# Causal attention before two expert layers: half-empty transposed blocks put together by two, and a first pair loaded in parts

## The chip, the cores and the metric

The kernel runs on one core of one Trainium2 chip. The metric is device time in microseconds (us); a lower number is better. One core has five engines with a queue each: PE (matmul), DVE (vector), ACT (scalar), POOL (GpSimd) and SP, which here only issues loads and stores.

## The reference

```
scores = q @ k.T / sqrt(64)            # 2 batches x 12 heads, 448 x 448, float32
scores = where(key > query, -1e9, scores)
attn   = exp(scores - max) / (sum + 1e-9)
x      = (attn @ v), heads side by side # 896 tokens x 768
x      = relu(x @ w_in)**2 @ w_out      # 768 -> 2048 -> 768
h      = x @ w_in2
out    = (h - tanh(h)) @ w_out2
```

## The kernel before

Attention goes by 12 **pairs** of heads (6 pairs a batch). The 448 queries and the 448 keys are cut into 7 blocks of 64. For query block `c` only keys 0 to c are computed, `64*(c+1)` columns, so the seven blocks of a pair have 64 to 448 columns. The two heads of a pair lie on the two halves of the 128 partitions.

`scores` (L264) makes a pair's scores in two steps of two banks (`STEPS`, L54). Its matmuls use a quarter of the array each (64 rows, 64 columns), and four run beside each other: head j takes row half j, and the two banks of a step take the two column halves, so in one bank of the two the heads lie exchanged (`TURNED`). `maxes` (L287, DVE) reads a block's scores, adds the mask, writes it to the SBUF tile `p` and takes the row maximum; `exps` (L305, ACT) makes the exponentials and their sums; `small`, `sums`, `recips`, `norms` (DVE) divide by the sum.

`transposes` (L335, PE) then turns `p` block by block, 128 keys x 64 queries x 2 heads at a time: query block c with 64*(c+1) keys takes one transpose for each begun 128 keys, 16 in all, of which the last of blocks 0, 2, 4 and 6 is half empty (zeros, written once at L252). They go into four PSUM banks of four, and `tcopy` (L342, ACT) copies each bank, 512 columns, to `pt`. `pv` (L348, PE) multiplies with the values: for each 128 keys one matmul a head over all query blocks that see them, 448, 320 and 192 columns with 128 rows, and 64 columns with 64 rows for the last keys. Two heads run beside each other on the two column halves. A float32 matmul shows as two passes in the trace. `xhi` (ACT) and `xlo` (DVE) take the result apart into `x`.

The order of the work is written out by hand: iteration s of the loop at L549 makes the scores of pair s, the norms of pair s-1, and transposes, copies and product of pair s-2, each engine strictly in the order of the code. From s = 8 on (`f`), PE also gets the first six groups of the first expert layer's matmuls for batch 0 (`fill`), 18 matmuls a pair. DVE and ACT take a weight's passes in between (`w_prep`: shift, merge, high, split on DVE, one `w_exp` on ACT, L107), by a budget of 700 a pair; `late` runs the ACT pass that a DVE pass put off. After the loop come the four matmul stages of the expert layers, three matmuls for each product (L387 to L389).

At the start, `load_qk(0)` sends q on SP's queue and k on ACT's, nine `warm` matmuls follow on PE, and SP loads pairs 1 and 2, all values of batch 0 with the last 64 keys of both batches (`vend`), and the first weight.

Of the kernel before, what the change touches and what calls it, by code (L numbers as in the profile page):

```python
# [52 lines left out]

STEPS = (((6,), (5, 0)), ((3, 2), (4, 1)))  # L54
SOFF = {6: 0, 5: 0, 0: 384, 3: 0, 2: 256, 4: 0, 1: 320}
SI = {c: i for i, c in enumerate(c for st in STEPS for cs in st for c in cs)}
TURNED = {c for st in STEPS for c in st[1]}
# [6 lines left out]
TBASE = {kc: TBLK.index((kc, 2 * kc)) for kc in range(4)}  # L64
# [3 lines left out]
def body(ctx: ExitStack, tc: tile.TileContext, qT, kT, vL, w1, w2, w3, w4, out):  # L68
# [5 lines left out]
    mask = sb.tile([P, S], F32, name="mask")  # L74
# [127 lines left out]
    def load_qk(n):  # L202
        if n < NPAIR:
            b, hp = divmod(n, NP)
            qk[n] = (tmp(f"q{n}"), tmp(f"k{n}", "w"))
            nc.sync.dma_start(out=qk[n][0], in_=qT[b, hp])
            (nc.scalar if n == 0 else nc.sync).dma_start(out=qk[n][1], in_=kT[b, hp])

    def load_v(b):
        t = sb.tile([P, 3, DM], F32, tag=f"v{b}", name=f"v{b}")  # L210
        nc.sync.dma_start(out=t, in_=vL[b, : 3 * P].rearrange("(t p) d -> p t d", p=P))
        if b == 0:
            vs["end"] = slot(7, [D, B, DM], F32, "vend")
            nc.sync.dma_start(out=vs["end"], in_=vL[:, 3 * P :].rearrange("b p d -> p b d"))
        vs[b] = [t[:, 0], t[:, 1], t[:, 2], vs["end"][:, b]]
# [10 lines left out]
    warm(9)  # L226
# [4 lines left out]
    for j in range(2):  # L231
        r = mask[D * j : D * j + D, S - D :]
        nc.gpsimd.affine_select(out=r, in_=r, compare_op=ALU.is_ge, fill=-8e9, base=0, pattern=[[-1, D]], channel_multiplier=1)
# [3 lines left out]
    load_v(0)  # L237
    w_load(0)
# [9 lines left out]
    prob = [slot(i, [P, 2048], F32, f"p{i}") for i in range(3)]  # L248
    for i in range(3):
# [10 lines left out]
    def step(n, t):  # L260

        return STEPS[1 - t if n == 0 else t]

    def scores(n, t):  # L264
        q, k = qk[n]
        banks = []
        for z, cs in enumerate(step(n, t)):

            tag, bufs = ("s", 4) if n != 1 else ("t", 2) if t == 0 else ("oh"[z], 1)
            bank = ps.tile([P, 512], F32, tag=tag, bufs=bufs, name=f"s{n}_{t}_{z}")  # L270
            banks.append(bank)
            for c in cs:
                sc[n, c] = bank[:, SOFF[c] : SOFF[c] + D * (c + 1)]
        for i in range(2):
            for z, cs in enumerate(step(n, t)):
                for c in cs[i : i + 1]:
                    for j in range(2):
                        r, e = slice(D * j, D * j + D), D * (j ^ z)
                        nc.tensor.matmul(sc[n, c][e : e + D], lhsT=q[r, D * c : D * c + D], rhs=k[r, : D * (c + 1)], start=(c == cs[0]), stop=(c == cs[-1]), skip_group_check=True)  # L279
        if t == 1:  # L280
            qk.pop(n)
            load_qk(n + 3)

    def blocks(n, t):
        return [c for cs in step(n, t) for c in cs]

    def maxes(n, t, part=slice(None)):  # L287
# [4 lines left out]
        for c in cs[part]:  # L292
# [4 lines left out]
                in1=mask[:, S - w :],  # L297
# [37 lines left out]
    def transposes(n, t):  # L335
        tag, bufs = ("h", 1) if t == 2 and n < NP else ("t", 2)
        bank = tb[n, t] = ps.tile([P, 512], F32, tag=tag, bufs=bufs, name=f"t{n}_{t}")
        for i, (kc, c) in enumerate(TBLK[4 * t : 4 * t + 4]):
            o = bank.rearrange("p (i j q) -> p i j q", j=2, q=D)[:, i, :: -1 if c in TURNED else 1]
            nc.tensor.transpose(o, prob[n % 3][:, POFF[c] + P * kc : POFF[c] + P * kc + P], ident)  # L340

    def tcopy(n, t):  # L342
        if t == 0:
            pt[n] = slot(3 + n % 2, [P, 16, P], F32, f"pt{n}")
# [3 lines left out]
    def pv(n, kcs):  # L348
        b, hp = divmod(n, NP)
        if 0 in kcs:  # L350
            ob[n] = ps.tile([P, 512], F32, tag="o", bufs=1, name=f"o{n}")
        o = ob[n]
        for kc in kcs:
            r = P if kc < 3 else D
            m = NQ - 2 * kc
            for j in range(2):
                h = 2 * hp + j
                nc.tensor.matmul(  # L358
                    o[D * j : D * j + D, P * kc : S],
                    lhsT=vs[b][kc][:r, D * h : D * h + D],  # L360
                    rhs=pt[n][:r, TBASE[kc] : TBASE[kc] + m, D * j : D * j + D],
                    start=(kc == 0),
                    stop=(kc == 3),
                    skip_group_check=True,
                )
        if 3 in kcs:
# [182 lines left out]
    for s in range(NPAIR + 2):  # L549
# [26 lines left out]
        late()  # L576
# [12 lines left out]
        if a >= 1:  # L589
            xlo(a - 1)  # L590
        if f and ss:
# [29 lines left out]
        if sa:  # L621
            pv(a, range(4))
        if not ss:
            pump()
        late()
        if s == 1:
            warm(5, "s", 4)
        if s in (2, 3):
            w_load(s - 1)
        if s == 4:  # L630
            load_v(1)
    xhi(NPAIR - 1)
# [57 lines left out]
```

## Time and profile before

| what | value |
|---|---|
| median of 3 runs | 554.47 us (553.4 to 555.22) |
| the profiled execution's own time | 554.28 us |
| its span in the profile | 552.4 us |
| PE busy | 544.5 us (99%) |
| DVE, ACT busy | 347.6 us (63%), 330.0 us (60%) |
| chain that ended last | PE 93%, ACT 6%, DVE 1% |

The span is what the instructions cover; the 1.9 us between it and the time lie around the program. The shares of busy time are means over stages that differ: the pairs of the first batch fill about the first 45 us, those of the second batch the time to about 100 us, and the expert layers the rest.

### The profile page before, as it was taken

What the parts mean: (1) busy time and instruction counts of PE and PEld (TensorE: products, weight loads), DVE (VectorE), ACT (ScalarE), POOL (GpSimd) and SP (SyncE); (2) the same over time, 40 slices, a digit from 0 to 9 for tenths busy, and PEclk for the clock granted to TensorE, in tenths of its full rate; (3) what the DMA queues carried; (4) which work ended last, traced back from release to release, by engine and by line L of the source; (5) the groups of instructions that cost most, each with busy time, mean ns of one, the idle gap of its engine ahead of it and who ended that gap; (6) DMA issues with size and microseconds to landing.
All of it is one profiled execution on the core that took longest, in us unless ns stands there. A gap on an engine that the chain in (4) does not pass through costs nothing.

```text
span 552.4 us, 7889 instructions
## 1 busy us (share of the span) xinstructions
PE 544.5 (99%) x3038; PEld 480.9 (87%) x3038; DVE 347.6 (63%) x742; ACT 330.0 (60%) x630; POOL 1.6 (0%) x9
## 2 busy tenths in 40 slices
PE   8999999999999999999999999999999999999997
PEld 4667777899999999999999999999999999999996
DVE  5999998364534244453554688987654588887311
ACT  6999987577424266665333388776553677865100
POOL 1000000000000000000000000000000000000000
PEclk9999999999999999999999999999999999999999
DMA  8844223353443333331324130113755301016111
GB/s 259 299 149 132 109 82 97 108 171 115 135 152 115 114 115 114 115 114 58 114 66 163 58 115 1 57 58 90 237 188 171 114 1 58 0 59 217 55 50 51
DMA packets 15525, 61.85 MB, mean 112 GB/s; under 512 B 1664, under 2 KB 6400, under 8 KB 15488
## 3 DMA queue, kind: packets, MB, share of 16 engines
q1 hardware_dynamic: 15200, 61.00, 33.2%
q8 instruction: 24, 0.39, 0.3%
q10 hardware_dynamic: 288, 0.34, 0.2%
q14 instruction: 13, 0.11, 0.1%
HBM read 58.59 MB, written 2.75 MB: 111 GB/s over the span
## 4 chain that ended last, share of the span: by engine, by line
PE 93%; ACT 6%; DVE 1%; issue 0%; DVEq 0%
PE h L387 14%; PE h L389 14%; PE h L388 14%; PE o L387 14%; PE o L388 14%; PE o L389 14%; ACT p L312 3%; PE o L358 3%; PE t L340 2%; PE s L279 2%; ACT pt L346 2%; PE warm L224 1%; ACT raw L107 0%; DVE p L294 0%; ACT x L371 0%; DVE p L333 0%
## 5 line engine op out<-in xcount | busy, mean ns | idle before, releaser
L387 PE MATMUL o<-g,w 128*128 128x448 f32 x384 | 140.4, 366 | 0.0
L388 PE MATMUL o<-g,w 128*128 128x448 f32 x384 | 140.4, 366 | 0.0
L389 PE MATMUL o<-g,w 128*128 128x448 f32 x384 | 140.2, 365 | 0.0
L387 PEld LDWEIGHTS o<-g,w 128*128 128x128 f32 x384 | 72.1, 188 | 6.1
L389 PEld LDWEIGHTS o<-g,w 128*128 128x128 f32 x384 | 72.1, 188 | 6.0
L388 PEld LDWEIGHTS o<-g,w 128*128 128x128 f32 x384 | 72.1, 188 | 5.8
L387 PE MATMUL h<-x,w 128*128 128x448 f32 x192 | 72.3, 377 | 0.0
L388 PE MATMUL h<-y,w 128*128 128x448 f32 x192 | 70.6, 368 | 0.0
L389 PE MATMUL h<-y,w 128*128 128x448 f32 x192 | 70.6, 368 | 0.0
L389 PE MATMUL h<-x,w 128*128 128x448 f32 x192 | 70.6, 368 | 0.0
L387 PE MATMUL h<-y,w 128*128 128x448 f32 x192 | 70.6, 368 | 0.0
L388 PE MATMUL h<-x,w 128*128 128x448 f32 x192 | 70.5, 367 | 0.0
L124 ACT CAST w<-raw 128x768 fp32r<-128x768 f32 x56 | 50.5, 903 | 26.9 <-DVE raw L121 26.9
L121 DVE SCALAR_TENSOR_TENSOR raw<-raw 128x768 int32<-128x768 int32 x64 | 61.1, 954 | 5.4 <-ACT raw L107 5.4
L107 ACT ACTIVATE raw<-raw 128x768 f32<-128x768 f32 x64 | 59.1, 923 | 0.0
L137 DVE TENSOR_TENSOR w<-raw,w 128x768 fp32r<-128x768 f32 x32 | 30.6, 957 | 35.0 <-ACT w L124 34.8
L400 DVE TENSOR_TENSOR g<-r,g 128x448 fp32r<-128x448 f32 x32 | 20.0, 625 | 48.0 <-ACT g L397 48.0
L527 ACT COPY part<-o 128x448 f32<-128x448 f32 x24 | 12.8, 534 | 57.0 <-PE o L389 57.0
L135 DVE SCALAR_TENSOR_TENSOR w<-w,raw 128x768 fp32r<-128x768 f32 x32 | 30.6, 956 | 23.3 <-ACT w L124 23.3
L312 ACT ACTIVATE p<-p,st 128x256 f32<-128x256 f32 (+6 forms) x84 | 40.8, 516 | 4.2 <-DVE st L294 4.2
L387 PEld LDWEIGHTS h<-x,w 128*128 128x128 f32 x192 | 36.1, 188 | 4.0 <-issue 0.7
L389 PEld LDWEIGHTS h<-y,w 128*128 128x128 f32 x192 | 36.0, 188 | 3.4
(57 smaller groups left out, 718.5 us busy)
## 6 DMA issues: line engine op xcount, KB each, us to landing
raw<-w SPq DMA_DIRECT2D x64, 768.0 KB, 4.3
q<-qT SPq DMA_DIRECT2D x12, 224.0 KB, 5.3
k<-kT SPq DMA_DIRECT2D x11, 224.0 KB, 3.8
out<-part SPq DMA_DIRECT2D x11, 224.0 KB, 1.9
v<-vL SPq DMA_DIRECT2D x2, 1152.0 KB, 7.7
vend<-vL SPq DMA_DIRECT2D x1, 384.0 KB, 11.4
k<-kT ACTq DMA_DIRECT2D x1, 224.0 KB, 3.5
out<-part ACTq DMA_DIRECT2D x1, 112.0 KB, 1.7
```

Of the source, the lines that this page charges most:

```text
L107: nc.scalar.activation(h, h, AF.Prelu, scale=2.0**-112, alpha=2.0**32)
L121: nc.vector.scalar_tensor_tensor(out=lo, in0=hi, scalar=3, in1=lo, op0=ALU.logical_shift_left, op1=ALU.bitwise_or)
L124: act_late.append(lambda: nc.scalar.copy(out=st["w"][:, 0], in_=lo.bitcast(F32)))
L135: nc.vector.scalar_tensor_tensor(out=w[:, 1], in0=w[:, 0].bitcast(F32), scalar=-(1.0 - 2.0**-24), in1=f, op0=ALU.mult, op1=ALU.add)
L137: nc.vector.tensor_sub(out=w[:, 1], in0=f, in1=w[:, 0])
L312: nc.scalar.activation(p, p, AF.Exp, bias=st[:, 0, i : i + 1], scale=-1.0, **kw)
L358: nc.tensor.matmul(o[D * j : D * j + D, P * kc : S], lhsT=vs[b][kc][:r, D * h : D * h + D], rhs=pt[n][:r, TBASE[kc] : TBASE[kc] + m, D * j ...
L387: nc.tensor.matmul(h, lhsT=hi, rhs=xh, start=(k == 0), stop=False)
L388: nc.tensor.matmul(h, lhsT=hi, rhs=xl, start=False, stop=False)
L389: nc.tensor.matmul(h, lhsT=lo, rhs=xh, start=False, stop=(k == kk - 1))
L400: nc.vector.tensor_sub(out=dst[1], in0=v, in1=dst[0])
L527: nc.scalar.copy(out=part[m][:, b], in_=o)
```

## The change

1. **Transposes.** Keys are laid out in the order 6, 0, 1, 2, 3, 5, 4 (`KEYS`), and `p` is packed (`POFF`) so that the diagonal block of query block 0 lies just ahead of that of block 6, and the one of block 2 ahead of that of block 4. One transpose then turns two diagonal blocks. 16 transposes become 14, the last copy 256 columns instead of 512, and the zeros (12 DVE memsets) go. The mask gets 256 more columns.
2. **Product.** The three long matmuls a head lose 64 columns each (384, 256, 128). The four diagonal blocks are multiplied apart (`pv_ends`), 64 columns and 64 rows each: two on the upper row half at once, two on the lower row half after the next pair's scores, behind a POOL memset (`token`) that waits for the upper ones and is waited for by the lower ones. `xhi` and `xlo` of the last pairs move accordingly, and the last two pairs' results get another bank.
3. **Scores.** Block 4 takes two matmuls a head (64 and 256 columns). The first pair goes in three steps, blocks (2 | 1, 0), (3 | 4), (6 | 5), and its loads in parts: the first 256 columns of q on SP and of k on ACT, the other 192 of both on ACT. Seven warm matmuls instead of nine.
4. **Loads and weight passes.** Batch 0's values come in two halves, the second after pair 4's q and k; the first weight's load moves behind pair 3's q and k. At the end of an iteration `late` runs only when no scores are left, so the ACT weight pass comes after the next pair's copies; in the `f` iterations the first `late` goes.

```diff
+STEPS0 = (((2,), (1, 0)), ((3,), (4,)), ((6,), (5,)))
+KPART = {c: ((0, D, D * (c + 1)),) for c in range(6)}
+KPART[4] = ((0, 6 * D, D), (D, D, 4 * D))
+KPART[6] = ((0, 0, S),)
-POFF = (0, 128, 256, 512, 768, 1152, 1536)
-TBLK = [(kc, c) for kc in range(4) for c in range(2 * kc, NQ)]
+FIRST = 256
+KEYS = (6, 0, 1, 2, 3, 5, 4)
+POFF = (0, 1024, 512, 1152, 704, 1408, 64)
+TBLK = [(kc, (c,)) for kc in range(3) for c in range(2 * kc + 1, NQ)]
+ENDS = ((0, 6), (2, 4))
+TBLK += [(None, cs) for cs in ENDS]
...
+            if n == 0:
+                c, r = slice(0, FIRST), slice(FIRST, S)
+                nc.sync.dma_start(out=qk[n][0][:, c], in_=qT[b, hp, :, c])
+                nc.scalar.dma_start(out=qk[n][1][:, c], in_=kT[b, hp, :, c])
+                nc.scalar.dma_start(out=qk[n][0][:, r], in_=qT[b, hp, :, r])
+                nc.scalar.dma_start(out=qk[n][1][:, r], in_=kT[b, hp, :, r])
...
-    warm(9)
+    warm(7)
...
-    load_v(0)
-    w_load(0)
+    load_v(0, 0, 2)
...
-            for c in range(0, NQ, 2):
-                e = POFF[c] + D * (c + 1)
-                nc.vector.memset(prob[i][:, e : e + D], 0.0)
...
+                        for o, a, w in KPART[c]:
+                            nc.tensor.matmul(sc[n, c][e : e + D, o : o + w], lhsT=q[r, D * c : D * c + D], rhs=k[r, a : a + w], start=(c == cs[0] and o == 0), stop=(c == cs[-1]), skip_group_check=True)
...
-        nc.scalar.copy(out=pt[n][:, 4 * t : 4 * t + 4], in_=bank.rearrange("p (i q) -> p i q", q=P))
+        e = min(4 * t + 4, NT)
+        nc.scalar.copy(out=pt[n][:, 4 * t : e], in_=bank.rearrange("p (i q) -> p i q", q=P)[:, : e - 4 * t])
...
+    def pv_ends(n, z):
+        for i, cs in enumerate(ENDS):
+            c = cs[z]
+            for j in range(2):
+                r, e = slice(D * z, D * z + D), D * (j ^ (c in TURNED))
+                ins = product(n, j, slice(D * c, D * c + D), c // 2, r, pt[n][r, NT - 2 + i, e : e + D], start=False, stop=(z == 1 and i == 1))
+                if z == 1 and i == j == 0:
+                    tc.add_manual_dep(ins, passed.pop(n), WAITS, reason="row tiles of one bank")
+        if z == 0:
+            p = nc.gpsimd.memset(token, 0.0).ins
+            tc.add_manual_dep(p, ins.name, WAITS, reason="row tiles of one bank")
+            passed[n] = p.name
...
         if ss:
-            scores(s, 0)
-            scores(s, 1)
+            for t in range(len(steps(s))):
+                scores(s, t)
+            if a >= 1:
+                pv_ends(a - 1, 1)
...
-        if a >= 1:
+        if a >= 1 and ss:
             xhi(a - 1)
+        if a == NPAIR - 1:
+            xhi(a - 2)
...
-        late()
+        if not f:
+            late()
...
-            pv(a, range(4))
+            pv(a)
+            if not ss:
+                pv_ends(a - 1, 1)
         if not ss:
             pump()
-        late()
+            late()
         if s == 1:
             warm(5, "s", 4)
+        if s == 0:
+            w_load(0)
+        if s == 1:
+            load_v(0, 1, 2)
...
+    pv_ends(NPAIR - 1, 1)
```

On PE, the product of pair 0 (`o`, from `pt` and the values `v` and `vend`) and the first scores of pair 3 (`s`), before:

```order
L358 MATMUL o_288<-pt_246,v_108 64x448 x2
L358 MATMUL o_288<-pt_246,v_108 64x320 x2
L358 MATMUL o_288<-pt_246,v_108 64x192 x2
L358 MATMUL o_288<-pt_246,vend 64x64 x2
L279 MATMUL s_0_0_301<-k_148,q_147 64x448 x2
```

and now:

```order
L386 MATMUL o_285<-pt_245,v_108 64x384 x2
L386 MATMUL o_285<-pt_245,v_108 64x256 x2
L386 MATMUL o_285<-pt_245,v_108 64x128 x2
L386 MATMUL o_285<-pt_245,v_108 64x64 x4
L306 MATMUL s_0_0_300<-k_139,q_138 64x448 x2
```

The two short matmuls at the end (one a head) became four, and the long ones have 192 columns a head less between them.

On PE, the end of the same scores and the first transposes of pair 1 (`t`), before:

```order
L279 MATMUL s_0_1_302<-k_148,q_147 64x64 x2
L279 MATMUL s_1_0_309<-k_148,q_147 64x256 x2
L279 MATMUL s_1_1_310<-k_148,q_147 64x320 x2
L279 MATMUL s_1_0_309<-k_148,q_147 64x192 x2
L279 MATMUL s_1_1_310<-k_148,q_147 64x128 x2
L340 MATMUL t_0_327<-ident,p_115 128x2x64 x2
L340 MATMUL t_0_327<-ident,p_115 128x128 x2
```

and now:

```order
L306 MATMUL s_1_1_309<-k_139,q_138 64x64
L306 MATMUL s_1_1_309<-k_139,q_138 64x256
L306 MATMUL s_1_1_309<-k_139,q_138 64x64
L306 MATMUL s_1_1_309<-k_139,q_138 64x256
L306 MATMUL s_1_0_308<-k_139,q_138 64x192 x2
L306 MATMUL s_1_1_309<-k_139,q_138 64x128 x2
L386 MATMUL o_285<-pt_245,vend 64x64 x2
L386 MATMUL o_285<-pt_245,v_108 64x64 x2
L374 MATMUL t_0_332<-ident,p_113 128x2x64
L374 MATMUL t_0_332<-ident,p_113 128x128 x2
```

The scores of 320 columns are cut in two, and four matmuls of pair 0's product now stand between the scores and the transposes.

On ACT, the exponentials (`p`) of pair 2, the first weight's pass (`raw`), the cast of pair 0's result (`x`) and the copies of pair 1, before:

```order
L312 ACTIVATE p_116,st_267<-p_116,st_267 128x320
L107 ACTIVATE raw_112<-raw_112 128x768
L312 ACTIVATE p_116,st_267<-p_116,st_267 128x128
L371 CAST x_66<-o_288 128x448
L346 COPY pt_332<-t_0_327 128x512
L346 COPY pt_332<-t_1_334 128x512
L346 COPY pt_332<-t_2_340 128x512
L346 COPY pt_332<-t_3_346 128x512
```

and now:

```order
L339 ACTIVATE p_114,st_264<-p_114,st_264 128x128
L418 CAST x_66<-o_285 128x448
L381 COPY pt_337<-t_0_332 128x512
L381 COPY pt_337<-t_1_339 128x512
L381 COPY pt_337<-t_2_345 128x512
L381 COPY pt_337<-t_3_351 128x256
L124 ACTIVATE raw_156<-raw_156 128x768
L339 ACTIVATE p_112<-p_112,st_357 128x64
```

The weight pass went from ahead of the last exponential to behind the copies, and the last copy is half as wide.

## Rows read from the trace of the kernel before

**Rows 1.** The page: its span, and the chain that ended last.

```profile
span 552.4 us, 7889 instructions
...
PE 93%; ACT 6%; DVE 1%; issue 0%; DVEq 0%
```

**Rows 2.** Windows: length, busy us (instructions) of PE, PEld, DVE, ACT, POOL; clock, DMA.

```profile
14.51:20.10 5.59, 4.98 (x56) 3.20 (x55) 5.33 (x27) 5.59 (x17) 0.00 (x0) 1.00 1.04 391
20.10:26.00 5.90, 5.90 (x64) 4.19 (x63) 5.74 (x25) 5.90 (x21) 0.00 (x0) 1.00 0.69 244
26.00:31.60 5.60, 5.46 (x60) 3.81 (x59) 5.60 (x27) 5.60 (x19) 0.00 (x0) 1.00 0.83 293
31.60:38.00 6.40, 6.40 (x71) 4.80 (x68) 5.69 (x28) 6.40 (x21) 0.00 (x0) 1.00 0.28 78
54.79:63.98 9.19, 9.19 (x81) 7.18 (x82) 8.30 (x31) 8.24 (x23) 0.00 (x0) 1.00 0.23 82
```

**Rows 3.** Chain of waits in order of time: start, length, what; the first pairs.

```profile
4.31 1.76 PE s L279 x16
6.15 0.42 DVE p L294
6.62 3.47 ACT p L312 x13
10.11 0.23 DVE st L318
...
20.64 1.93 ACT pt L346 x4
22.57 3.34 ACT p L312 x13
```

**Rows 4.** The same chain, in the second batch and at its end.

```profile
54.79 1.97 PE o L358 x14
56.82 1.52 PE s L279 x18
...
59.16 0.87 PE t L340 x8
...
86.70 0.41 ACT x L371
```

**Rows 5.** Timeline at 87 us: start, length, instruction, [idle before <- releaser].

```profile
87.65 1.14 PE L340 MATMUL t<-ident,p 128*128 128x128 f32 x8 [0.34 <-ACT pt L346]
```

**Rows 6.** DMA from 2.7 to 3.9 us: rate, and each queue's packets, MB and share.

```profile
DMA packets 293, 0.47 MB, mean 390 GB/s; under 512 B 32, under 2 KB 293, under 8 KB 293
...
q1 hardware_dynamic: 149, 0.24, 52.9%
q10 hardware_dynamic: 144, 0.23, 50.1%
```

**Rows 7.** Groups by line and shape: busy us, mean ns of one.

```profile
L346 ACT COPY pt<-t 128x512 f32<-128x512 f32 x48 | 25.3, 598 | 3.7 <-PE t L340 3.7
L312 ACT ACTIVATE p<-p,st 128x448 f32<-128x448 f32 x12 | 8.2, 684 | 0.0
L371 ACT CAST x<-o 128x448 fp32r<-128x448 f32 x12 | 6.3, 523 | 0.0
L312 ACT ACTIVATE p<-p,st 128x64 f32<-128x64 f32 x12 | 4.3, 369 | 0.0
```

**Rows 8.** Timeline of PE from 54.7 us: a pair's product and the scores after it.

```profile
54.72 1.84 PE L358 MATMUL o<-pt,v 128*64 128x448 f32 x12
56.49 0.27 PE L358 MATMUL o<-pt,vend 64*64 64x64 f32 x2
...
56.59 0.23 PE L358 MATMUL o<-pt,vend 64*64 64x64 f32 x2
56.65 1.69 PE L279 MATMUL s<-k,q 64*64 64x448 f32 x26
```

**Rows 9.** Timeline of the first 9 us: the warm matmuls on PE.

```profile
0.77 3.52 PE L224 MATMUL warm<-const-bfloat16-1.0 128*128 128x448 bf16 x9 [0.77 <-PEq L683]
...
8.20 1.13 PE L224 MATMUL warm<-const-bfloat16-1.0 128*128 128x448 bf16 x5
```

More of the change, by code (lines that the diff above doesn't have):

```diff
@@ L205, in load_qk, with load_v @@
             qk[n] = (tmp(f"q{n}"), tmp(f"k{n}", "w"))
[L206 to L215, printed above, removed]
+            if n == 0:
[4 more added lines that the diff above has]
+                nc.scalar.dma_start(out=qk[n][1][:, r], in_=kT[b, hp, :, r])
+            else:
+                nc.sync.dma_start(out=qk[n][0], in_=qT[b, hp])
+                nc.sync.dma_start(out=qk[n][1], in_=kT[b, hp])
+    def load_v(b, part=0, parts=1):
+        if b not in vs:
+            t = sb.tile([P, 3, DM], F32, tag=f"v{b}", name=f"v{b}")
+            if b == 0:
+                vs["end"] = slot(7, [P, B, DM], F32, "vend")
+            vs[b] = [t[:, 0], t[:, 1], t[:, 2], vs["end"][:, b], t]
+        w = DM // parts
+        d = slice(part * w, part * w + w)
+        nc.sync.dma_start(out=vs[b][4][:, :, d], in_=vL[b, : 3 * P, d].rearrange("(t p) d -> p t d", p=P))
+        nc.sync.dma_start(out=vs["end"][D:][:, b, d], in_=vL[b, 3 * P :, d])
     load_qk(0)
@@ L258, in body, with steps, score_bank @@
     ob = {}
-    def step(n, t):
-        return STEPS[1 - t if n == 0 else t]
+    def steps(n):
+        return STEPS if n else STEPS0
+    def score_bank(n, t, z):
+        if (n, t) in ((0, 2), (1, 0)):
+            return ("oh"[z], 1) if n == 0 else ("t", 2)
+        return "s", 4
     def scores(n, t):
@@ L266, in scores @@
         banks = []
-        for z, cs in enumerate(step(n, t)):
-            tag, bufs = ("s", 4) if n != 1 else ("t", 2) if t == 0 else ("oh"[z], 1)
+        off = SOFF if n else SOFF0
+        for z, cs in enumerate(steps(n)[t]):
+            tag, bufs = score_bank(n, t, z)
             bank = ps.tile([P, 512], F32, tag=tag, bufs=bufs, name=f"s{n}_{t}_{z}")
@@ L272, in scores @@
             for c in cs:
-                sc[n, c] = bank[:, SOFF[c] : SOFF[c] + D * (c + 1)]
+                sc[n, c] = bank[:, off[c] : off[c] + D * (c + 1)]
         for i in range(2):
-            for z, cs in enumerate(step(n, t)):
+            for z, cs in enumerate(steps(n)[t]):
                 for c in cs[i : i + 1]:
@@ L284, in blocks @@
     def blocks(n, t):
-        return [c for cs in step(n, t) for c in cs]
+        return [c for st in (steps(n)[1:] if t else steps(n)[:1]) for cs in st for c in cs]
     def maxes(n, t, part=slice(None)):
@@ L366, in pv @@
-        if 3 in kcs:
+        h = 2 * hp + j
+        return nc.tensor.matmul(ob[n][D * j : D * j + D, o], lhsT=vs[b][kc][rows, D * h : D * h + D], rhs=rhs, skip_group_check=True, **flags).ins
+    def pv(n):
+        tag, bufs = ("o", 1) if n < NPAIR - 2 else ("s", 4)
+        ob[n] = ps.tile([P, 512], F32, tag=tag, bufs=bufs, name=f"o{n}")
+        for kc, i in enumerate(TBASE):
+            m = NQ - 2 * kc - 1
+            for j in range(2):
+                product(n, j, slice(S - D * m, S), kc, slice(0, P), pt[n][:, i : i + m, D * j : D * j + D], start=(kc == 0), stop=False)
+        pv_ends(n, 0)
```

68 lines of the change are left out of this document (37 added, 31 removed).

## The prediction

> **What bounds the kernel now.** I read the chain of waits first. It runs 93% of the span on PE and 6% on ACT [rows 1]: the ACT part is the first batch's pairs, the rest is PE. The windows say the same by stage [rows 2]. In the four stretches of one pair each from 14.51 to 38.00 us ACT is busy for all of 23.49 us, DVE for 22.36, and PE in one of them for 5.46 of 5.60: three engines nearly full at once. In the second batch (54.79 to 63.98 us, one pair) PE is busy for all 9.19 us, DVE for 8.30 and ACT for 8.24. So until about 45 us an edit counts by what it takes from ACT, if DVE and PE can follow; from there to about 100 us by what it takes from PE; behind that nothing is edited. At the front, ACT starts its first exponential at 6.62 us, after scores that wait for the loads until 4.31 [rows 3], and hardly stops again: time won there is kept.
>
> The sum is made against the profiled execution, 554.28 us with a span of 552.4. The median of the three runs is 0.19 us above it, which no comparison of this kernel can tell. About 0.3%, 1.7 us, is what a measurement can tell from no change.
>
> **The start.** Before, q and k of pair 0 come on two queues that share 390 GB/s evenly, 0.24 and 0.23 MB in the same 1.2 us [rows 6]. The first parts leave 192 of 448 columns of k (98 KB) for later; at half the rate that is 0.50 us, so the scores start near 3.8 us instead of 4.31. Seven warm matmuls instead of nine, at 0.39 us each (3.52 for 9 [rows 9]), end near 3.5 us and are not in the way. Step 0 has 192 columns a tile where the first step had 448 in 1.76 us [rows 3]: 0.75 us. The first maximum then starts near 4.65 us (6.15 before) and the first exponential near 5.1 (0.47 later, as between the rows of DVE and ACT [rows 3]).
>
> But steps 1 and 2 wait for the second parts, 196 KB on ACT's queue beside SP's loads. If the queues share bytes evenly they take 1.0 us more and land near 4.8 us. If they take turns by packet, each of 256 packets of 768 B waits for one of 1,792 B, and 256 x 2,560 B at 390 GB/s is 1.7 us: 5.5 us. The rows show equal packets only and can't tell the two. The Trainium skill, "DMA: Bandwidth & Descriptors", section on queues, rings and completion order, says that a DMA engine takes turns between queues a packet at a time; by it the later landing holds, and the sum would be 0.5 us worse than the one below. No row here confirms it.
>
> Step 1 (320 columns at the first step's pace, 1.26 us) then ends at 6.1 to 6.8 us, and step 2 (448 columns, between 0.76 us, half of the 1.52 us of a later pair's scores [rows 4], and 1.76) at 6.8 to 8.5 us. From there a maximum and the two widest exponentials (0.55 and about 1.35 us, the second from 684 ns for 448 columns [rows 7]) end pair 0 at 8.7 to 10.4 us. Before it was 10.1 (6.62 + 3.47 [rows 3]), and DVE's sums waited for it. So -1.4 to +0.3 us; I take **-0.5**, near the middle. The zero memsets and the wider mask lie before 6 us on engines that wait there: nothing. Two more DMA issues on ACT only delay the table load, which has until 5 us.
>
> **The copies.** Four copies take 1.93 us in the chain [rows 3], and one 598 ns [rows 7]. Half a copy saves 256 columns. The exponentials' slope, (684 - 369) ns over 384 columns, makes that 0.21 us, and the slope between the cast of 448 columns and the copy of 512, (598 - 523) over 64, 0.30 [rows 7]. I take 0.24 a pair, and six pairs lie where ACT is full: -1.4 us at most. DVE has 1.13 us to spare over four stretches [rows 2], 0.28 a pair, just over 0.24, and PE's round is about as long as ACT's. With engines this even some of it is lost in waits: **-0.9 us**, range -1.4 to 0. The weight passes that move behind the copies stay on ACT, 0.8 us each, and ACT stays full: nothing. The loads that move back are needed iterations later, and pair 3's q and k now go ahead of them.
>
> **PE in the second batch.** Eight transposes take 0.87 us [rows 4], so two fewer save 0.22 us a pair, 1.3 us in six pairs. Against that stands the product [rows 8]. The long matmuls lose 192 columns. A pair's scores have 896 columns a tile in 1.52 us [rows 4], 1.7 ns a column, so -0.33 us. The short ones grow from 2 passes to 8, two heads beside each other. In the rows the first short pass takes 0.10 us until the second starts (56.49 to 56.59), the second 0.06 until the scores follow on the same tile (56.65). The first has the change of tile shape in it, so I take 0.06: six more are +0.36, with 0.10 it would be +0.60. The lower half's four may run beside the end of the scores, as the scores now begin beside the last short passes: down to -0.2 net. Net +0.03 a pair, range -0.2 to +0.27, and 0.02 (0 to 0.06) for block 4's second matmul. Six pairs: -1.3 + 0.3 = **-1.0 us**, range -2.5 to +0.7. The lower half's wait for POOL's memset has a pair's scores, 1.5 us, to hide in.
>
> The Trainium skill, "TensorEngine Tiling (Array Packing)", speaks against this part: under instruction overhead, a matmul of up to 60 columns costs about as much as one of 60 and a small dimension isn't worth cutting, and under key properties, a change of tiling mode drains the array. Its 60 cycles beside the 64 columns of each pass would put the six added passes at 0.3 us more, an estimate from the page, and this part near +0.8. The row of 0.06 us for a pass of 64 columns (0.053 us at 2.4 GHz) doesn't bear that out.
>
> **A wait that goes.** At 87.65 us PE sat idle for 0.34 us on a copy [rows 5], and ACT's cast of x, 0.41 us in the chain just before it [rows 4], moves an iteration later: **-0.34**, range -0.41 to 0. **The end of attention.** After the last product the lower short passes of pairs 10 and 11 follow without scores between. Pair 11's wait for POOL has only pair 10's four passes, 0.24 us, as cover. No row shows such a round; DVE follows PE by 0.08 us (6.07 to 6.15 [rows 3]), so two hops and a memset may take 0.3: **+0.1**, range 0 to 0.5. The casts of pairs 10 and 11 have a whole group of 18 matmuls to hide behind.
>
> **Sum:** -0.5 - 0.9 - 1.0 - 0.34 + 0.1 = -2.6 us: a span of 549.8, a time of 551.7 us.
>
> **Rivals.** *Three even engines.* ACT's gain turns into waits for DVE or PE, so the copies bring nothing, the start -0.2, PE -0.5, the wait at 87 us stays: -0.6, 553.7 us. For it: the even fill of rows 2. Against it: DVE's 0.28 us a pair. Chance 0.20.
>
> *A slower start.* Nine warm matmuls took 0.39 us each and the five at 8.20 us 0.23 [rows 9]: PE ran near its lower level, 1.2 GHz, before it rose to 2.4 GHz, though the windows' clock column says 1.00 for the stretches shown. Now PE pauses between the warm matmuls and step 0 and again before step 1. If the rise comes later, step 2 and pair 1's scores run at half pace, and the start costs +0.8 instead of -0.5: -1.3, 553.0 us. Chance 0.12.
>
> *Short products cost more than they save*, the rival on the other side. Each added pass takes the full 0.10 us, none runs beside scores, and the turns from scores to short passes and back cost 0.10 us each: -0.33 + 0.60 + 0.20 + 0.06 = +0.53 a pair against 0.22 from the transposes. That is +0.31 x 6 = 1.9 us in the second batch, and with PE's round at 5.46 of 5.60 us [rows 2] about +0.2 in each of five pairs before; the start 0, the end +0.5: +3.4, 557.7 us. It decides once passes and turns cost more than 0.55 us a pair. Chance 0.08.
>
> **How the numbers follow.** My forecast has 0.60 and its own range is 549.6 to 553.2. The range of 8 in 10 takes in the even engines and the slow start: 549.6 to 554.4. Faster by over 0.3% means below 552.8 for the execution read here: most of the forecast, four tenths of the slow start, a tenth of the even engines, 0.64 in all. Slower means nearly all of the third rival, 0.07. The rest, 0.29, is within 0.3%.
>
> **What would show it.** First exponential near 5.1 us; pair 0's last one by 9.6. Pairs of the first batch about 5.5 us apart instead of 5.7, with ACT still full. Second-batch pairs at 9.0 instead of 9.19 us; 14 transposes at 0.109 us; short passes 0.06 us apart, and the scores begun 0.2 us earlier after the product. No PE wait near 85 us. I am wrong if short passes stand 0.10 us or more apart, if PE waits for POOL behind the scores, or if step 1 starts after 5.5 us.

## The result and the profile after

The changed kernel takes **549.36 us** (median of 4 runs, 548.44 to 549.62) against 554.17 us of the kernel before on the same chip: a ratio of 0.9911 (95% interval 0.9895 to 0.9927). The forecast was 551.7 us with a range from 549.6: the direction was right, and the time lies 0.24 us below the range. The profiled execution took 549.62 us.

The page of the changed kernel, its span and the shares of the chain that ended last (of the kernel before: [rows 1]):

```profile
span 547.8 us, 8250 instructions
...
PE 92%; ACT 6%; DMA 1%; ACTq 0%; issue 0%; DVE 0%; DVEq 0%; POOLq 0%
```

A DMA has come into the chain. The chain of waits of the changed kernel in order of time (start, length, what), the front:

```profile
1.65 4.68 DMA k<-kT
6.32 0.04 issue
6.37 5.66 PE s L306 x44
12.03 1.26 PE warm L251 x5
13.29 2.20 PE s L306 x28
...
17.96 3.33 ACT p L339 x13
```

Against [rows 3] this is the first surprise. k's second part lands at 6.33 us, steps 1 and 2 and pair 1's scores then take 5.66 us, and the first row of four copies comes late. ACT's timeline (start, length, instruction) of the first, the second and the fifth row, before:

```profile
13.73 0.56 ACT L346 COPY pt<-t 128x512 f32<-128x512 f32 x1
14.51 1.56 ACT L346 COPY pt<-t 128x512 f32<-128x512 f32 x3 [0.21 <-PE t L340]
...
20.54 2.03 ACT L346 COPY pt<-t 128x512 f32<-128x512 f32 x4
...
38.41 2.06 ACT L346 COPY pt<-t 128x512 f32<-128x512 f32 x4
```

And the changed kernel:

```profile
16.12 1.84 ACT L381 COPY pt<-t 128x512 f32<-128x512 f32 x4 [0.57 <-PE t L374]
...
21.59 1.84 ACT L381 COPY pt<-t 128x512 f32<-128x512 f32 x4
...
38.97 1.84 ACT L381 COPY pt<-t 128x512 f32<-128x512 f32 x4
```

In the kernel before, the 14.51 us at which the first window of [rows 2] begins is the second copy of its row; the first is at 13.73. Like points are the ends of the two rows: 16.07 us before (14.51 + 1.56), 17.96 now.

The windows of the changed kernel (columns as in [rows 2]), four rounds of the first batch and one pair of the second:

```profile
16.12:21.70 5.58, 5.53 (x77) 4.29 (x76) 5.54 (x29) 5.58 (x19) 0.25 (x1) 1.00 0.85 283
21.70:28.00 6.30, 6.03 (x81) 4.79 (x79) 6.20 (x27) 6.30 (x21) 0.10 (x1) 1.00 0.68 211
28.00:33.45 5.45, 4.95 (x71) 3.74 (x70) 5.45 (x27) 5.45 (x19) 0.46 (x1) 1.00 0.96 326
33.45:38.97 5.52, 5.47 (x77) 4.17 (x76) 5.52 (x27) 5.52 (x20) 0.46 (x1) 1.00 0.29 86
55.52:64.53 9.01, 9.01 (x94) 7.42 (x96) 8.31 (x31) 8.10 (x24) 0.16 (x1) 1.00 0.27 87
```

ACT is still full, and a pair of the second batch takes 9.01 us (9.19 before). The sum of the four rounds, 22.85 us, can't be set beside the 23.49 of [rows 2]: those windows leave out a copy and hold two weight passes, these hold one. From the second row of copies to the fifth, with one weight pass in each kernel, it is 17.87 us before (20.54 to 38.41) and 17.38 now: 0.16 us a round. So far the kernel is about as fast as before: +1.9 us to the end of the first row, then -0.9 to the first matmul of the expert layers (the first `fill`), then -1.5 to the end of the last product. The rest, 4.1 us, comes where nothing was edited. One of the three lines that issue the expert layers' matmuls, its instructions in the second group's first layer (h) and second layer (o): durations in ns (smallest/median/largest), first and last start. Before:

```profile
L387 PE MATMUL h<-x,w x96: 364/368/371, 195.9 to 254.4; 128*128 128x448 f32 x96
L387 PE MATMUL o<-g,w x96: 358/365/373, 255.0 to 313.0; 128*128 128x448 f32 x96
```

The changed kernel, the same view:

```profile
L434 PE MATMUL h<-x,w x96: 363/363/364, 194.8 to 251.8; 128*128 128x448 f32 x96
L434 PE MATMUL o<-g,w x96: 358/367/370, 252.4 to 310.6; 128*128 128x448 f32 x96
```

From the first to the last of 96 lie 95 x 3 matmuls. In h, 58.5 us or 205.3 ns each became 57.0 us or 200.0 ns; in o, 58.0 (203.5 ns) became 58.2 (204.2 ns). PE waits for nothing in either. The 1,044 h matmuls behind attention make that -5.5 us, 1,152 o matmuls +0.8 to +1.2: -4.3 to -4.7 us, near the 4.1 that the span shows.

The chains by stage, with two of the experiments below (`e2_before_pad32`: old attention, the changed kernel's matmul paces; `e4_whole_loads`: the change without the loads in parts), in us:

| | before | e2 | after | e4 |
|---|---|---|---|---|
| first row of copies ends | 16.07 | 16.15 | 17.96 | 15.59 |
| from there to the first fill | 33.01 | 33.04 | 32.12 | 32.15 |
| first fill to the end of the last product | 51.26 | 50.87 | 49.80 | 49.80 |
| expert layers behind it | 452.1 | 447.7 | 448.0 | 448.0 |
| span | 552.4 | 547.8 | 547.8 | 545.5 |

### The profile page after: what moved, and what is told of

Its sections match the earlier page's. It is cut to its first block, busy times and chain, and to the rows that moved or that the text cites. A ratio compares the mean times of both kernels' runs of the same rounds, so it can differ in the third digit from the quotient of the medians.

```text
span 547.8 us, 8250 instructions
## 1 busy us (share of the span) xinstructions
PE 539.7 (99%) x3204; PEld 484.6 (88%) x3204; DVE 345.9 (63%) x730; ACT 327.5 (60%) x630; POOL 4.3 (1%) x21
## 4 chain that ended last, share of the span: by engine, by line
PE 92%; ACT 6%; DMA 1%; ACTq 0%; issue 0%; DVE 0%; DVEq 0%; POOLq 0%
PE o L436 14%; PE o L435 14%; PE o L434 14%; PE h L434 14%; PE h L436 14%; PE h L435 14%; ACT p L339 3%; PE s L306 3%; PE o L386 2%; ACT pt L381 2%; PE t L374 2%; DMA k<-kT 1%; ACT raw L124 0%; ACT x L418 0%; PE warm L251 0%
## 5 line engine op out<-in xcount | busy, mean ns | idle before, releaser
L434 PE MATMUL h<-x,w 128*128 128x448 f32 x192 | 71.5, 372 | 0.0
L434 PE MATMUL h<-y,w 128*128 128x448 f32 x192 | 69.7, 363 | 0.0
L436 PE MATMUL h<-y,w 128*128 128x448 f32 x192 | 69.6, 362 | 0.0
L436 PE MATMUL h<-x,w 128*128 128x448 f32 x192 | 69.5, 362 | 0.0
L435 PE MATMUL h<-x,w 128*128 128x448 f32 x192 | 69.4, 362 | 0.0
L435 PE MATMUL h<-y,w 128*128 128x448 f32 x192 | 69.1, 360 | 0.0
L339 ACT ACTIVATE p<-p,st 128x320 f32<-128x320 f32 (+6 forms) x84 | 41.0, 516 | 4.7 <-DVE st L321 4.6
```

Source lines behind the costliest of these rows:

```text
L339: nc.scalar.activation(p, p, AF.Exp, bias=st[:, 0, i : i + 1], scale=-1.0, **kw)
L434: nc.tensor.matmul(h, lhsT=hi, rhs=xh, start=(k == 0), stop=False)
L435: nc.tensor.matmul(h, lhsT=hi, rhs=xl, start=False, stop=False)
L436: nc.tensor.matmul(h, lhsT=lo, rhs=xh, start=False, stop=(k == kk - 1))
```

## Experiments

Each time is a median beside runs of the kernel before (554.13 to 554.24 us) on the same chip.

### Place in memory: three runs

The new 4-byte tile `token` takes 32 bytes a partition, and `p`, `pt` and `mask` changed size. So the weights and the slots of `g` (the second layers' moving tiles, which reuse `p`, `pt` and `vend`) begin elsewhere. Theory PLACE: the matmuls' pace goes by where moving tile and weights lie.

```diff
 # e1, on the changed kernel: weights and four of the eight g slots 32 bytes further
-    token = sb.tile([P, 1], F32, name="token")
+    token = sb.tile([P, 16], F32, name="token")
 # e2, on the kernel before, behind the p tiles
+    nc.gpsimd.memset(sb.tile([P, 1], F32, name="pad"), 0.0)
 # e3: as e1, and two pads as in e2, the first ahead of x, so that x, g and weights all lie at multiples of 64
```

> The changed kernel with the token tile 64 bytes a partition instead of 4, which moves every tile allocated behind it (the weights w and some of the g tiles) by 32 bytes and nothing else. Theory PLACE (the expert layers' matmuls read x, g and w at a pace that hangs on where these tiles lie, and the 32 bytes of the token moved w to 32 beyond a multiple of 64, where x lies too): the first-layer matmuls go back from 200.0 to about 205.3 ns apart, the second-layer ones from 204.4 to about 203.3, and the time rises by about 4.3 us to 553.7. Rival WORK (the pace came from what DVE, ACT and DMA do beside PE, which changed with the order of the passes): spacing stays 200.0 and 204.4, time 549.4.

> The kernel before with a tile of 4 bytes (32 in the layout) put behind the three p tiles, which moves w and some g tiles by 32 bytes. PLACE: first-layer matmuls 200.0 ns apart instead of 205.3, second-layer ones near 204.4 instead of 203.3, time about 4.3 us lower than before, 549.9. WORK: no change, 554.2.

> The changed kernel with pads that put x, w and all g tiles on multiples of 64 bytes. PLACE in the form that the moving tile and the weights want the same remainder by 64: first-layer matmuls 200.0 ns apart as in the changed kernel, and second-layer ones 203.3 as in the kernel before (there all at multiples of 64), about 1.2 us better than the changed kernel, 548.2. PLACE in the form that w alone wants remainder 32: 205.3 ns and 553.7. WORK: 549.4.

Measured: e1 553.26 us (ratio 0.9979, 0.9964 to 0.9994), e2 549.53 (0.9905, 0.9872 to 0.9938), e3 549.34 (0.9905, 0.9874 to 0.9935). One idle tile of 4 bytes makes the kernel before 4.7 us faster; 60 more bytes of `token` cost the changed one 3.9 us. The view of one line's matmuls, e2:

```profile
L388 PE MATMUL h<-x,w x96: 363/363/364, 194.9 to 252.0; 128*128 128x448 f32 x96
L388 PE MATMUL o<-g,w x96: 358/367/370, 252.6 to 310.8; 128*128 128x448 f32 x96
```

And e1:

```profile
L434 PE MATMUL h<-x,w x96: 369/369/370, 194.7 to 253.6; 128*128 128x448 f32 x96
L434 PE MATMUL o<-g,w x96: 360/365/369, 254.2 to 311.7; 128*128 128x448 f32 x96
```

e2 has the paces of the changed kernel, to a tenth of a us over the 96; e1 has 206.7 ns in h and 201.8 in o, not the 205.3 and 203.3 of the kernel before that were expected. PLACE is shown, but not the form that e3 tried: by the remainder of 64 its h matmuls should have stood 200.0 or 205.3 ns apart, and they stand 202.8. At equal places (e2 has the same remainders by 256 of all addresses as the changed kernel) the attention of the change is worth 549.53 - 549.36 = 0.17 us, nothing measurable.

### The loads in parts: e4, e6, e12

```diff
 # e4, on the changed kernel
-                c, r = slice(0, FIRST), slice(FIRST, S)
...
+                nc.sync.dma_start(out=qk[n][0], in_=qT[b, hp])
+                nc.scalar.dma_start(out=qk[n][1], in_=kT[b, hp])
...
-    warm(7)
+    warm(9)
 # e6, on the changed kernel, ahead of pair 0's second step
+        if (n, t) == (0, 0):
+            warm(8, "t", 2)
 # e12, on e5 (below): parts, q's on SP and k's on ACT, ahead of all other loads; warm(7)
+                for h in (c, r):
+                    nc.sync.dma_start(out=qk[n][0][:, h], in_=qT[b, hp, :, h])
+                    nc.scalar.dma_start(out=qk[n][1][:, h], in_=kT[b, hp, :, h])
```

> The changed kernel with the first pair's q and k loaded whole again and nine warm matmuls, three score steps kept. Theory PARTS COST (the second parts land at 6.3 us and hold up steps 1 and 2, and the pause delays the rise of the PE clock, which costs the 1.6 us by which the first full row of copies starts later than before): first scores at 4.3, that row of copies by 14.5 us instead of 16.1, time 1.5 us lower, 547.9. Rival HIDDEN (ACT or DVE hold the first pairs anyway): within 0.4 us of 549.4.

> The changed kernel with its loads in parts, and eight more warm matmuls between the first and the second step of pair 0, in the 1.9 us in which PE waits for the second parts. All places in memory are as in the changed kernel (549.36 us). Theory CLOCK (the pause keeps the clock at its lower level until about 12 us, and that costs most of the 2.3 us that whole loads won): steps 1 and 2 and pair 1's scores run at the higher level from about 6.5 us on, the first row of four copies starts near 14.6 us instead of 16.1, time 547.5 to 548. Rival LANDING (the late second parts hold pair 0 whatever the clock is): the copies start at 15.5 us or later, time 548.8 to 549.4; if the warm matmuls run past the landing they add up to 0.5 us.

> The kernel with every distance at 64 and whole first loads (544.14 us), with pair 0's loads in parts again, but q's second part on SP's queue and k's on ACT's, each directly behind its first part and so ahead of all other loads; seven warm matmuls as in the changed kernel. Theory QUEUE (the parts cost because the second ones, all on ACT's queue in 768-byte packets, shared the engines with pairs 1 and 2): the second parts land by 4.8 us, steps 1 and 2 follow step 0 with under 0.5 us of wait, the first exponential starts near 5.0 us, four copies near 13.5 us: 543.7 to 544.2 us. Rival PAUSE (any wait of PE between the steps keeps the clock low): copies at 14.5 us or later, 544.9 us or more. Rival SMALL PACKETS (768 bytes a packet are slow by themselves): the second parts land at 5.3 us or later.

Measured: e4 547.09 us (0.9864, 0.9836 to 0.9891), e6 548.46 (0.9898, 0.9883 to 0.9913), e12 544.10 (0.9819, 0.9804 to 0.9834; e5, with whole loads, 544.14). The parts cost the change 2.3 us. Two causes show. PE's timeline of the changed kernel (start, length, instructions, [idle before <- releaser]):

```profile
3.56 0.92 PE L306 MATMUL s<-k,q 64*64 64x192 f32 x12
6.37 5.66 PE L306 MATMUL s<-k,q 64*64 64x256 f32 x52 [1.89 <-DMA k<-kT]
```

And that of e6:

```profile
3.66 0.92 PE L306 MATMUL s<-k,q 64*64 64x192 f32 x12
4.51 2.37 PE L251 MATMUL warm<-const-bfloat16-1.0 128*128 128x448 bf16 x8
7.10 3.00 PE L306 MATMUL s<-k,q 64*64 64x256 f32 x52 [0.23 <-DMA k<-kT]
```

The same 52 matmuls take 5.66 us behind a pause of 1.89 us and 3.00 us behind warm matmuls: nearly the ratio of the two clock levels, 1.2 and 2.4 GHz, although the windows give a granted clock of 1.00 (third value from the end) for both stretches, in the changed kernel and in e6:

```profile
6.40:12.00 5.60, 5.60 (x53) 3.91 (x54) 3.34 (x15) 3.41 (x12) 0.00 (x0) 1.00 0.83 260
```

```profile
7.10:10.00 2.90, 2.90 (x52) 2.17 (x52) 2.20 (x11) 1.73 (x7) 0.00 (x0) 1.00 0.86 246
```

That it was the clock is read from the pace of the matmuls alone. In e6 the load came 0.74 us later still (5.42 us in its chain, 4.68 after), and its copies start at 15.11 us, 1.0 earlier than in the changed kernel and 1.4 later than with whole loads: CLOCK is shown as a mechanism, and LANDING, the late parts themselves, holds the rest. Why it lands late, in the DMA view of the changed kernel from 3.7 to 6.2 us (rate; each queue's packets, MB, share; q1 is SP's, q10 ACT's):

```profile
DMA packets 579, 0.77 MB, mean 308 GB/s; under 512 B 63, under 2 KB 579, under 8 KB 579
...
q1 hardware_dynamic: 412, 0.66, 81.8%
q10 hardware_dynamic: 167, 0.11, 15.4%
```

ACT's queue gets 14% of the bytes beside pairs 1 and 2. In e12 only the first parts stand ahead of the second ones, one of each on either queue, and the loads of pairs 1 and 2 come behind; the same view of e12's first 8 us (KB each, us from issue to landing):

```profile
k<-kT ACTq DMA_DIRECT2D x1, 96.0 KB, 3.0
q<-qT SPq DMA_DIRECT2D x1, 96.0 KB, 2.8
```

3.0 us instead of 4.7 (the same k part after): QUEUE holds, SMALL PACKETS falls. PAUSE falls too, in PE's timeline of e12:

```profile
6.52 1.81 PE L306 MATMUL s<-k,q 64*64 64x448 f32 x32 [0.88 <-DMA k<-kT]
```

PE has done pair 0's three steps before this pause of 0.88 us, and pair 1's 32 passes behind it are not slow. The first exponential starts at 4.85 us and the copies at 13.13, but e5's start at 13.30 with whole loads (the runs with whole loads have 13.01 to 13.75, so single executions differ by more than that). Pair 1's k, which now comes later, is what PE waits for next (its chain has a DMA of k until 6.38 us). So done well, parts win nothing measurable.

### What the pairing of the blocks is worth: e7 to e10

```diff
 # e7, on e4: the lower short products at once
             pv(a)
+            pv_ends(a, 1)
...
 # e8, on e4: both calls of late() as in the kernel before
-        if not f:
-            late()
+        late()
...
-            late()
+        late()
 # e9, on e4: two more transposes in the fourth bank
+        if t == 3:
+            for i in (2, 3):
+                nc.tensor.transpose(bank[:, P * i : P * i + P], src, ident)
 # e10: as e9, and the fourth copy takes the whole bank
-        e = min(4 * t + 4, NT)
+        e = 4 * t + 4
...
+            pt[n] = slot(3 + n % 2, [P, 16, P], F32, f"pt{n}")
```

> The changed kernel with whole first loads (547.09 us), and the short products of the lower half directly behind the product in place of behind the next pair's scores. What the scores cover is then bare: PE waits for the token, a memset of 0.25 us on POOL and two semaphores, in each pair. If the prediction's estimate of 0.3 us for the hops and the memset holds, +0.3 us in each of six pairs of the second batch and, where PE is as full as ACT, in part of the first batch's: +1.8 to +3 us, 549 to 550 us. If the hops take longer (0.6 us), +4 to +6 us. If the lower four passes also lose the overlap with the scores, 0.2 us a pair more. Rival: the scheduler's slack takes it, +0.5 us or less.

> The changed kernel with whole first loads (547.09 us), and the first batch's weight passes on ACT put back to where they were, ahead of the last exponentials and behind the products. The prediction costed this edit at nothing: they stay on ACT, which is full either way: 547.1 us within 0.3, the rounds of the first batch as long as before. Rival ORDER (a pass ahead of an exponential delays DVE's sums and with them PE's transposes): 0.2 to 0.4 us a pair in the five pairs of the first batch, 548 to 549 us.

> The changed kernel with whole first loads (547.09 us), and in the fourth bank of each pair two more transposes, whose result nobody copies: the PE part of the pairing is undone alone. Theory of the prediction (two transposes are 0.22 us a pair, and in the second batch PE sets the pace): second-batch pairs 9.23 us instead of 9.01, the round without pairs' scores before the end the same, +1.3 us over six pairs, and where PE is as full as ACT a little in the first batch: 548.4 to 548.9 us. Rival SLACK (they hide behind the waits of the last copy): 547.1 to 547.6 us.

> As the run with two more transposes, and the fourth copy takes all 512 columns again: the PE part and the ACT part of the pairing are undone together. Places modulo 128 are those of the changed kernel. Theory of the prediction (0.24 us of copy a pair, of which 0.15 comes through in six pairs): rounds of the first batch 5.6 to 5.7 us instead of 5.45 to 5.5, 0.9 us (0 to 1.4) above the run with transposes alone: 549.3 us, range 548.4 to 550.3. Rival EVEN ENGINES (ACT's time turns into waits for DVE or PE): no difference between the two runs.

Measured (e4: 547.09): e7 **551.37** us (0.9953, 0.9939 to 0.9968), e8 547.69 (0.9886, 0.9871 to 0.9901), e9 548.61 (0.9898, 0.9883 to 0.9913), e10 549.22 (0.9911, 0.9896 to 0.9925).

e7 is the cover's price. PE's timeline of e7 in the second batch:

```profile
54.54 1.89 PE L383 MATMUL o<-pt,v 128*64 128x384 f32 x20
56.72 0.33 PE L383 MATMUL o<-pt,vend 64*64 64x64 f32 x4 [0.28 <-POOL token L407]
```

The bare wait is 0.28 us, as the prediction estimated for the end, but a pair comes to 9.45 us instead of 9.01, +0.44; that the other 0.16 us are the four passes, which no longer run beside scores, is likely and not shown. From the copies to the first fill e7 takes 2.2 us more than e4, from there to the last product 2.5: more than the whole attention gain, and above the 549 to 550 us expected for the bare wait alone; with the 0.2 us a pair named there for the lost overlap it comes near.

e8 ends its span at 545.6 us against e4's 545.5, and the intervals overlap. But its first row of copies ends 0.72 us earlier than e4's, in the spread of starts told above, and that hides what the edit does. The windows from the end of the first row to the first fill (columns as above), e4:

```profile
15.59:47.74 32.15, 30.52 (x428) 23.58 (x425) 31.69 (x143) 32.15 (x105) 1.48 (x6) 1.00 0.63 205
```

And e8:

```profile
14.87:47.80 32.93, 30.54 (x428) 23.69 (x424) 31.67 (x143) 32.72 (x105) 1.47 (x6) 1.00 0.61 203
```

DVE's wait for ACT in the same stretch of e8 (us in total, times, longest):

```profile
DVE st L346 <- ACT p L336: 1.3, 2, 0.7
```

The stage is 0.78 us longer, and in the changed kernel it is 32.12 us with a much later start. ACT is no longer full, and DVE waits 1.3 us for exponentials that stand behind the weight passes (0.3 in e4). So moving the weight passes is worth about 0.8 us in the first batch, by one execution of each: ORDER, not nothing. e9 takes 51.05 us from the first fill to the end of the last product against 49.80, +0.21 a pair; the transposes were costed at 0.22. In e10 the five rounds from the first copy to the product of the first batch's last pair take 31.41 us against e9's 30.67: the fourth copy is worth 0.15 a round, the figure taken in the prediction. From the end of the first row to the first fill e9 takes 32.40 us and e10 32.93. The medians of e9 and e10 differ by 0.6 us with overlapping intervals, so this last number rests on the profiles.

### The rule of the place, and the fastest version: e5, e11, e13, e14

Three pads and a larger `token` set the distances; no instruction of the work changes. e11 and e14 move the weights 32 bytes further.

```diff
 # e5 on e4; e13 on e12 has 56, 32 and 48, 16; e11 on e5 has 24, 32, 24, 8; e14 on e12 56, 32, 56, 8
+    nc.gpsimd.memset(sb.tile([P, 24], F32, name="pad0"), 0.0)
-    token = sb.tile([P, 1], F32, name="token")
+    token = sb.tile([P, 32], F32, name="token")
+            if n == 1:
+                nc.gpsimd.memset(sb.tile([P, 16], F32, name="pad1"), 0.0)
+            nc.gpsimd.memset(sb.tile([P, 16], F32, name="pad2"), 0.0)
```

> The changed kernel with the first pair's q and k loaded whole, as in the run before (547.09 us), and four pads that move tiles: every moving tile (x and all eight slots of g) then starts 32 behind a multiple of 128 bytes and every weight tile 96 behind one, so the distance from moving tile to weights is 64 modulo 128 in both layers of both expert blocks. Theory DISTANCE 128 (the pace of a 448-column matmul goes by that distance modulo 128: 0 gave about 202.6 ns, 32 about 205.4, 64 about 200.0, 96 about 206.6): the second layers go from 204.3 to 200.0-201.8 ns, 1152 matmuls, -2.9 to -5.0 us: 542.1 to 544.2 us; the first layers stay at 200.0. Rival HALF (only the remainder by 64 of each tile counts, same half good or bad): the run with all tiles at multiples of 64 had 202.7 and 201.9; the second layer would come to about 202, and the first would rise to 202.7: 547 us. Rival OTHER (the second layer is paced by the accumulators and not by the place of g): 547.1 us, nothing changes.

> The kernel with every distance at 64 (544.14 us), and the weights 32 bytes further on, so that every distance from moving tile to weights is 96 modulo 128. No instruction changes. Theory DISTANCE 128: the first layers go from 200.0 to 206.6 ns and the second from 201.8 to 206.6 or 208: +6.9 us (1044 matmuls behind attention) and +5.5 to 7 us (1152): 556 to 558.5 us, slower than the kernel before. Rival HALF (only the remainder by 64 counts): weights at multiples of 64 and g at 32 were never better or worse than any other mix: 544 to 549 us.

> The run with parts on both queues (544.10 us) with six of the eight slots of g moved by 128 bytes, so that the distance from moving tile to weights, now counted modulo 256, is 192 for x and for every slot of g. Over all runs so far the paces by that distance are: 0: 202.7 ns, 64: 202.4, 96: 200.0, 128: 203 to 206, 160: 205.4, 192: 200.0 to 201, 224: 206.6. Theory DISTANCE 256: the second layers go from 201.8 to 200.0 to 200.6 ns, 1152 matmuls, -1.4 to -2.1 us: 542.0 to 542.7 us; the first layers stay at 200.0. Rival SLOT (the second layer has a cost of its own of about 1.8 ns, from the accumulators' eight groups or the slots' own places): 544.1 us, no change.

> The same kernel with the weights 32 bytes further on and two slots of g kept in place, so that every distance is 224 modulo 256. No instruction changes. Theory DISTANCE 256: 206.6 ns in both layers, against 200.0 and 200.0 to 200.6: +6.9 us (1044 matmuls behind attention) and +7 us (1152): 556 to 557 us, slower than the kernel before, though its attention is over 2 us faster. Rival DISTANCE 128 with an exception (what the run at 96 modulo 128 showed in its second layers): 549 to 551 us. Rival SLOT: the first layers alone slow down, 551 us.

Measured: e5 544.14 us (0.9823, 0.9806 to 0.9839; the upper end of what was expected), e11 551.35 (0.9951, 0.9939 to 0.9962), **e13 541.78** (0.9777, 0.9762 to 0.9792), e14 551.94 (0.9970, 0.9952 to 0.9988). The view of one line's matmuls, e11:

```profile
L434 PE MATMUL h<-x,w x96: 363/369/369, 193.1 to 251.9; 128*128 128x448 f32 x96
L434 PE MATMUL o<-g,w x96: 362/363/369, 252.6 to 310.1; 128*128 128x448 f32 x96
```

e13:

```profile
L436 PE MATMUL h<-x,w x96: 362/364/364, 190.8 to 247.8; 128*128 128x448 f32 x96
L436 PE MATMUL o<-g,w x96: 362/363/364, 248.4 to 305.4; 128*128 128x448 f32 x96
```

e14:

```profile
L436 PE MATMUL h<-x,w x96: 367/368/368, 193.1 to 251.4; 128*128 128x448 f32 x96
L436 PE MATMUL o<-g,w x96: 367/368/368, 252.0 to 310.3; 128*128 128x448 f32 x96
```

The built programs give the addresses. Moving rows are 1,792 bytes and more, weight tiles 6,144, their blocks 512, all multiples of 256, so the distance from moving tile to weights modulo 256 is one number for each slot:

| run | x to weights | h, ns | g slots to weights | o, ns |
|---|---|---|---|---|
| before | 160 | 205.3 | 128 and 0 | 203.5 |
| after, e2 | 192 | 200.0, 200.4 | 160 and 0 | 204.2 |
| e1 | 224 | 206.7 | 192 and 0 | 201.8 |
| e3 | 0 | 202.8 | 192 and 0 | 201.8 |
| e5 | 192 | 200.4 | 64 (2 slots 192) | 201.8 |
| e11 | 224 | 206.3 | 96 (2 slots 224) | 201.8 |
| e13 | 192 | 200.0 | 192 | 200.0 |
| e14 | 224 | 204.6 | 224 | 204.6 |

Modulo 128, as first thought, e11's second layers should have gone to 206 ns and stayed at 201.8: that rule fell. Modulo 256 it is in line: with each matmul of the trace put to its slot by the built program, e11's six slots at 96 take 200.3 ns and its two at 224 take 205.9, so 96 is as fast as 192. e13, forecast from the rule at 542.0 to 542.7 us, came to 541.78: 192 is fast in all eight slots. e14 slowed both layers, as that rule and no other said, but to 204.6 ns and not to 206.6; its time missed the expected 556 us by 4 and lies nearer to the 549 to 551 us of the two rivals, so that only the view by layer speaks for the rule. The distance sorts fast from slow and is not the whole rule: x and the weights have the same remainders by 256 in e1, e11 and e14, and h takes 206.7, 206.3 and 204.6 ns. 32 was not tried.

## Why the prediction was right or wrong

**The sentence that failed most: "behind that nothing is edited".** It was true of the instructions and false of the time: 4.1 of the 4.6 us by which the span shrank lie there. The change's tiles moved the others, and the paces of 2,304 matmuls followed. The diff shows the new tile and the sizes; no term was made for them.

**The start, -0.5 (-1.4 to +0.3): wrong in sign, +1.9 at the end of the first row of copies.** First scores at 3.56 us, first exponential at 5.03, as forecast (3.8 and 5.1). The step that failed is the landing of the second parts, put between 4.8 and 5.5 us: 6.33. Step 1 starts at 6.37, past the 5.5 us that the prediction gave as a sign of being wrong, and pair 0's last exponential starts at 10.36, not by 9.6. Both bounds assumed an even share, of bytes or of turns; the view from 3.7 to 6.2 us has 167 packets against 412, at 308 GB/s and not 390. The Trainium skill's sentence on turns, "DMA: Bandwidth & Descriptors", queues, rings and completion order, erred less, since the landing was the later one, but the counts of the view's packets are not one for one. The second failure came on top: the rival *a slower start* named the mechanism, with 0.12 and +0.8 us; e6 shows it. The prediction set the windows' clock column of 1.00 beside it, and in the start that column doesn't follow the pace. What the parts add to the change is +2.4 us (copies from 16.12 us against 13.75 in e4). The three steps alone, with whole loads, end the first row 0.5 to 1.2 us earlier than the kernel before (at 14.85 to 15.59 us in e4, e5, and e7 to e10, against 16.07), up to 0.2 of it by the shorter last copy.

**The copies, -0.9 (-1.4 to 0): right in size, -0.9, and only in part in its reason** (33.01 to 32.12 us from the end of the first row to the first fill). A round lost 0.16 us, where 0.15 was taken, and e10 gives 0.15. But the term put the move of the weight passes at nothing, and with them where they were (e8) the stage takes 32.93 us, almost as long as before: there the gain turns into waits of DVE for ACT, which is what *Three even engines* said. The copies' gain comes through because the weight passes moved; with them moved, that rival falls. The four windows of [rows 2] are one pair each only roughly: the first begins a copy late and the last ends 0.41 us before the fifth row; that ACT is full in them stands.

**PE in the second batch, -1.0, and the wait at 87 us, -0.34: together right.** At the changed kernel's paces (e2 against after) the stage from first fill to last product lost 1.07 us; 1.24 was the forecast with the end's +0.1. That a pair takes 9.01 us, as forecast, is in part luck: in e2 it takes 9.13 and not 9.19, by the pace of its `fill` matmuls, so the change is worth 0.12 us a pair where 0.17 was taken. Chain of the changed kernel in the second batch and at its end (for [rows 4] and [rows 5]):

```profile
55.52 1.76 PE o L386 x17
...
58.90 0.26 PE o L386 x6
...
59.97 0.87 PE t L374 x8
62.05 0.66 PE t L374 x6
...
86.84 0.48 ACT pt L381
87.36 0.92 PE t L374 x6
```

PE's timeline at the end of attention:

```profile
99.43 0.33 PE L386 MATMUL o<-pt,vend 64*64 64x64 f32 x4 [0.26 <-POOL token L410]
```

The 14 transposes are 0.109 us each, and e9 returns 0.21 a pair. Product and scores, from the product's start to the first fill, went from 3.55 us (54.79 to 58.34 [rows 4]) to 3.64: +0.09 where +0.03 was taken. By the prediction's estimate from the 60 cycles of the Trainium skill's "TensorEngine Tiling (Array Packing)", instruction overhead, it would be some +0.3 a pair (six times 60 cycles are 0.15 us at 2.4 GHz; 0.3 is what they are at 1.2 GHz); the trace stands nearer the row. *Short products cost more than they save* falls in this order of the work, but e7 shows how near it was: without the scores as cover a pair costs 0.44 us more. The wait at 87 us has shrunk and not gone: ACT's cast is out of the chain, but PE's transposes still follow ACT's copy, 0.42 us after the start of the matmul ahead of them (86.94 us) where it was 0.70 (86.95 to 87.65). At the end PE waits 0.26 us for POOL, in the range of 0 to 0.5.

**The sum.** -2.6 us for the attention came out for the change without its parts: e4 against e2 is 547.09 - 549.53 = -2.44, though the -0.5 us in it had been worked out for loads in parts. With them it is -0.17, and places gave the other 4.6. The forecast of "faster" came true by luck, for a reason it didn't have.

## What to carry to other kernels

When a change adds a tile or changes a tile's size, compare the pace of long runs of untouched matmuls first: here one 4-byte tile was worth more than the whole edit, and in this kernel pads that put every moving tile 192 bytes modulo 256 before its weights, with the change, made 541.78 us, 2.2% below the kernel before. Test an edit's gain at equal addresses, with a pad in the old kernel. Where engines are nearly even, an edit's gain can hang on the order of other work: take stages from like point to like point, since the totals of e4 and e8 hid it. A load split in parts cost 2.3 us here, with its second parts beside other pairs' loads, and won nothing measurable with them ahead; look at what PE does in the wait, since behind 1.89 us of idling its matmuls ran at half pace here.

## What the runs showed of the hardware that was not expected

- A 448-column float32 matmul pass started every 200.0 to 206.7 ns by the place of its operands alone, with PE never idle (table above). The Trainium skill, "TensorE: Matmul & The Clock Gate", Part 2, says that PE's two read ports keep the loading of weights from taking bandwidth from the running matmul; a pace that depends on the distance between the two operands speaks against full independence. What in the memory does it, no run here shows.
- The granted clock read 1.00 for 5.66 us in which 52 score matmuls went at about half the pace that they had in e6.
- A POOL memset of one column shows 0.10 to 0.46 us in the changed kernel (spans on POOL are rough): the windows above have 0.25, 0.10, 0.46, 0.46 and 0.16 for one each. PE's bare wait for it in e7, hops included, is 0.28 us.
